# Attention tiles of a fused transformer block: residual rows moved from the GpSimd queue to the SyncE queue, weight loads paced by the attention tile before

## The chip, the cores and the metric

One Trainium2 chip, of which the kernel uses one core. The metric is the time of one execution on the device in microseconds (us); where several executions are shown, it is their median.

## The reference

One transformer block on 2048 tokens of width 1024, batch 1, weights and activations in bf16: a layer norm, linear attention with 32 heads of 32, a residual addition, a second layer norm, a gated MLP of width 3584, a second residual addition.

```
phi = lambda t: where(t > 0, t + 1, exp(t)) + 1e-6
q, k, v = heads(layernorm(x) @ wqkv)             # 32 heads of 32
kv = einsum("bhsd,bhse->bhde", phi(k), v);  z = phi(k).sum(s)
o  = (phi(q) @ kv) / (phi(q) . z + 1e-6)
h  = x + o @ wo
g  = layernorm(h) @ W_gate;  u = layernorm(h) @ W_up
out = h + (relu(g) * u) @ W_down
```

## The kernel before

The kernel runs through four stages. (1) K, V and the sums over tokens, to about 122 us: 16 tiles of 128 tokens are loaded, normalised, transposed by DMA and multiplied. (2) Q, the attention tiles and the first quarter of the MLP's up side (four column blocks for half of the tokens), to about 299 us. (3) The rest of gate and up, to about 585 us. (4) The down projection and the output. The large products use Strassen's scheme, seven products of blocks in place of eight, so the vector engine forms sums of input and weight blocks (`left_sums`, L113 to L120, and `weight_sums`, L606 to L620).

The change is in stage 2. `attn_stages(t)` (L497) makes five steps for one tile of 128 tokens:

- `nd` (L503 to L520): eight small matmuls (L511) give numerators and denominators, ACT inverts the denominators (L515, L517), DVE multiplies into `o_sb` (L518, three pieces for a tile).
- `oT` (L522 to L525): SyncE issues a DMA transpose of `o_sb`.
- `x_in` (L527 to L530): the tile's 128 rows of x (256 KB) are loaded into `x_res`, for the residual addition.
- `wo_h` (L532 to L557): sixteen matmuls with `wo` (L541), DVE adds x to them in place and sums the rows (L543, two pieces), the finished rows h are stored to `h_dram` (L546, 256 KB), DVE and ACT make mean and variance (L551 to L556; L553 is the pass that squares) and the normalised rows `hn` (L557).
- `hn_T` (L559, L560): SyncE issues a DMA transpose of `hn` into the operand of the MLP's matmuls. After tiles 4 to 7 and 12 to 15 `left_sums` follows on DVE.

The steps of different tiles overlap: `LAG = (0, 1, 1, 2, 4)` says by how many tiles each step trails `nd`. I number the tiles 0 to 15 in the order in which they run; oT(n), x(n), st(n) and hnT(n) are the transpose of `o_sb`, the load of x, the store of h and the transpose of `hn` of tile n.

Buffers set waits. `x_res` has three buffers (`XB = 3`), so x(n+3) may be issued only when st(n) has landed and L557 of tile n has read the buffer. `hn` has two (`HB = 2`), so the first pass over tile n+2 (L553) waits until hnT(n) has landed. `o_sb` has two.

The weights of the MLP's first four blocks, 4 MB in eight loads of 512 KB, arrive in the same stretch. `early_loads` (L486, issued by SyncE) are paced: before each, GpSimd copies one element of an `o_sb` into the destination (`hold`, L142), so that the load can't be issued before DVE has written that tile's `o_sb`. Step 1 issues two loads, steps 2 to 7 one each:

```
        if step:
            for _ in range(-(-len(early_loads) // (QSTEPS - step))):
                early_loads.pop(0)(held[step][0:1, 0:1])
```

The order on the engines is made by a scheduling framework: the program is recorded step by step, and the framework puts each engine's instructions into one fixed order, by its own estimate of when each could run. Every engine, and every engine's DMA issue queue, then works through its list in order: an instruction that waits holds up all behind it. So a changed issue engine can move instructions on other engines too.

Of the kernel before, what the change touches and what calls it, by code (L numbers as in the profile page):

```python
# [31 lines left out]
def block_kernel(ctx: ExitStack, tc: tile.TileContext, x, wqkv, wo, wg, wu, wd, out, H: int):  # L32
    nc = tc.nc
    P = 128
    xf = x.flatten_outer_dims()
# [35 lines left out]
    h_dram = [[dram.tile([P, NT, D], BF16, name=f"h_dram{i}_{s}") for s in range(NS)] for i in range(2)]  # L71
# [140 lines left out]
    with ExitStack() as actx:  # L212
# [208 lines left out]
        for c in range(KC):  # L421
            bnk, i = divmod(c, GPB)
# [54 lines left out]
    def load_group(g):  # L477

        tiles, loads = [], []
        for nm, v in (("wg", wg_v), ("wu", wu_v)):  # L480
            w_sb = wpools[g % 2].tile([P, KC, 2, GP * P], BF16, tag=nm, name=nm)
            for h in range(2):
                def load(after=None, w_sb=w_sb, v=v, h=h):
                    if after is not None:
                        hold(w_sb[0:1, 0, h, 0:1], after)
                    nc.sync.dma_start(out=w_sb[:, :, h, :], in_=v[:, :, h, g * GP * P:(g + 1) * GP * P])  # L486
                loads.append(load)
            tiles.append(w_sb)
        return tiles, loads

    early, early_loads = zip(*[load_group(g) for g in range(NE // GP)])
    early_loads = [f for loads in early_loads for f in loads]
    pieces = [(c, min(GPB, KC - c)) for c in range(0, KC, GPB)]

    held = []

    def attn_stages(t):  # L497

        i, r = divmod(t * P, HS)
        s, r = divmod(r, SW)  # L500
        st = {}

        def nd():  # L503
            o_sb = bwork.tile([P, D], BF16, tag="o_sb", name="o_sb")
            st["o"] = o_sb
            held.append(o_sb)
            ov = o_sb[:].rearrange("p (k h e) -> p k h e", k=KC, h=HPC)
            for c0, n in pieces:
                ps = ndpool.tile([P, NW], FP32, tag="ab", name="nd")
                for c in range(c0, c0 + n):  # L510
                    nc.tensor.matmul(ps[:, (c - c0) * NDW:(c - c0 + 1) * NDW], lhsT=pqT[:, c, t * P:(t + 1) * P],  # L511
                                     rhs=kvz[:, c, :], start=True, stop=True)
                ndv = ps[:, 0:n * NDW].rearrange("p (k w) -> p k w", w=NDW)
                den = bsmall.tile([P, GPB, HPC], FP32, tag="den", name="den")
                nc.scalar.activation(out=den[:, 0:n], in_=ndv[:, :, P:NDW], func=ACT.Ln, bias=deps[:], scale=1.0)  # L515
                rd = bsmall.tile([P, GPB, HPC], FP32, tag="rd", name="rd")
                nc.scalar.activation(out=rd[:, 0:n], in_=den[:, 0:n], func=ACT.Exp, scale=-1.0)  # L517
                nc.vector.tensor_tensor(  # L518
                    out=ov[:, c0:c0 + n], in0=ndv[:, :, 0:P].rearrange("p k (h e) -> p k h e", h=HPC),
                    in1=rd[:, 0:n, :].unsqueeze(3).to_broadcast([P, n, HPC, Dh]), op=ALU.mult)  # L520

        def oT():  # L522
            oT = bwork.tile([P, D], BF16, tag="oT", bufs=XB, name="oT")
            st["oT"] = oT[:].rearrange("p (c t) -> p c t", c=KC)
            nc.sync.dma_start_transpose(out=st["oT"], in_=st["o"][:])  # L525

        def x_in():  # L527
            x_sb = bwork.tile([P, D], BF16, tag="x_res", bufs=XB, name="x_res")
            nc.gpsimd.dma_start(out=x_sb[:], in_=xf[t * P:(t + 1) * P, :])
            st["x"] = x_sb  # L530

        def wo_h(borrow):  # L532
            h_sb = st["x"]
            tot = bsmall.tile([P, 2], FP32, tag="tot", name="tot")
            for j in range(2):
                if borrow:
                    ps = pspool.tile([P, NW], FP32, tag="E", bufs=2, name="attn")
                else:
                    ps = abpool.tile([P, NW], FP32, tag="ab", name="attn")
                for c in range(KC):  # L540
                    nc.tensor.matmul(ps[:], lhsT=st["oT"][:, c, :], rhs=wo_sb[:, c, j * NW:(j + 1) * NW],  # L541
                                     start=(c == 0), stop=(c == KC - 1))
                nc.vector.scalar_tensor_tensor(out=h_sb[:, j * NW:(j + 1) * NW], in0=ps[:], scalar=1.0,  # L543
                                               in1=h_sb[:, j * NW:(j + 1) * NW], op0=ALU.mult, op1=ALU.add,
                                               accum_out=tot[:, j:j + 1])
            nc.gpsimd.dma_start(out=h_dram[i][s][:, r // P, :], in_=h_sb[:])  # L546
            st["hn"] = bwork.tile([P, D], BF16, tag="hn", bufs=HB, name="hn")

            sm = bsmall.tile([P, 6], FP32, tag="sm", name="sm")
            nmean, var, lnv, rstd, nmr = (sm[:, i:i + 1] for i in range(5))  # L550
            nc.vector.tensor_scalar(out=nmean, in0=tot[:, 0:1], scalar1=tot[:, 1:2], scalar2=-1.0 / D,  # L551
                                    op0=ALU.add, op1=ALU.mult)
            nc.scalar.activation(out=st["hn"][:], in_=h_sb[:], func=ACT.Square, bias=nmean, scale=1.0, accum_out=var)  # L553
            nc.scalar.activation(out=lnv, in_=var, func=ACT.Ln, bias=LN_EPS, scale=1.0 / D)
            nc.scalar.activation(out=rstd, in_=lnv, func=ACT.Exp, scale=-0.5)
            nc.scalar.activation(out=nmr, in_=nmean, func=ACT.Identity, scale=rstd)  # L556
            nc.scalar.activation(out=st["hn"][:], in_=h_sb[:], func=ACT.Identity, bias=nmr, scale=rstd)  # L557

        def hn_T():  # L559
            nc.sync.dma_start_transpose(out=hnT[s][i][:, :, r:r + P], in_=st["hn"][:])  # L560

        return nd, oT, x_in, wo_h, hn_T

    LAG = (0, 1, 1, 2, 4)
# [5 lines left out]
    def attn_step(step):  # L570
        for k in range(len(LAG)):
            n = step - LAG[k]
            if n in begin_at:
                n = begin_at.index(n)
                if k == 3:
                    stages[n][k](QSTEPS <= step < STS + LAG[-1])
                else:
                    stages[n][k]()
                if k == len(LAG) - 1 and n % STS >= NT:
                    left_sums(hnT[n // STS], hns[n // STS], slice(n % NT * P, (n % NT + 1) * P), nc.vector)  # L580

    rest = [p for s in range(1, NS) for c in range(0, KH, 2) for p in [q_unit(s, c)] * 6]
    for step in range(QSTEPS):
        now = rest[step * len(rest) // QSTEPS:(step + 1) * len(rest) // QSTEPS]
        if step == QSTEPS - 1:
            while now:
                next(now.pop(0))
        attn_step(step)
        if step:
            for _ in range(-(-len(early_loads) // (QSTEPS - step))):  # L590
                early_loads.pop(0)(held[step][0:1, 0:1])
        for p in now:
            next(p)
    q1ctx.close()
# [285 lines left out]
    for r, (wt, f, fi, toks) in enumerate(runs):  # L880
        w = [ops() for _, ops in now]
        later = []
        for n, s in enumerate(toks):
# [51 lines left out]
            if k == nwin - 3:  # L935
                for x in range(2):
                    t = wpools[1].tile([P, KC * 2 * GP * P], BF16, tag=("wg", "wu")[x], name="wd")
# [16 lines left out]
    for n in range(2):  # L954
        t = fpool.tile([P, 4 * D], BF16, tag="wraw", bufs=2, name="xd")
# [242 lines left out]
    for n in range(1, len(OUTER)):  # L1198
# [73 lines left out]
        else:  # L1272
            pss = []
            for p in range(4):
# [13 lines left out]
                s, t0 = divmod(2 * p, NT)  # L1288
# [11 lines left out]
@with_exitstack  # L1300
def kernel(
    ctx: ExitStack,
    tc: tile.TileContext,
    A_x: bass.AP,
    A_wqkv: bass.AP,
    A_wo: bass.AP,
    B_x: bass.AP,
    B_W_gate: bass.AP,
    B_W_up: bass.AP,
    B_W_down: bass.AP,  # L1310
    out: bass.AP,
):
    block_kernel(tc, A_x, A_wqkv, A_wo, B_W_gate, B_W_up, B_W_down, out, H=32)
# [30 lines left out]
```

## Time and profile before

| | |
|---|---|
| median of 3 runs | 750.96 us (750.52 to 752.11) |
| the profiled execution | 750.52 us, its span 748.7 us |
| TensorE (PE) busy | 723.2 us, 97% of the span |
| VectorE (DVE), ScalarE (ACT), GpSimd (POOL) busy | 563.1, 322.4, 23.1 us |
| PE busy in 0 to 30 / 30 to 150 us | 25.63 / 117.07 us |
| PE busy in 150 to 290 us | 127.02 of 140 us |
| PE busy in 290 to 613 us | 321.60 of 323 us |
| x of the attention tiles, from GpSimd's queue | 16 loads of 256 KB, median 4.5 us to landing |
| h stores, from GpSimd's queue | 16 of 256 KB, median 3.5 us |
| oT and hnT, from SyncE's queue | 16 each, median 5.0 and 4.8 us |

How to read it: the matmuls fill the span almost everywhere. Time can be gained or lost only where PE has idle time or where something that PE waits for is late. In the attention stretch, between 150 and 290 us, PE is idle for about 13 us. After it, from 290 to 613 us, PE is idle for 1.4 us, so what that stretch loses or gains goes through to the end. The times from issue to landing include waiting behind other transfers on the 16 DMA engines.

### The profile page before, as it was taken

The numbers are of one execution on the slowest core, as the hardware profiler recorded it, in microseconds if no ns is written. First come the engines' busy times: TensorE is split into PE (matmuls) and PEld (weight loads), VectorE is DVE, ScalarE is ACT, GpSimd is POOL, SyncE is SP. The second block draws the span as 40 slices with busy tenths as digits, with TensorE's granted clock in tenths as the row PEclk, the third lists the DMA queues.
The fourth block names the chain that finished last, engine by engine and source line by source line (L and its number), as shares of the span: only waits on it lengthen the run. The fifth ranks groups of instructions, "written<-read, shape, count | busy, mean of one in ns | idle before, by whom it ended". The sixth has DMA issues, their size and how long they took to land.

```text
span 748.7 us, 10599 instructions
## 1 busy us (share of the span) xinstructions
PE 723.2 (97%) x3967; PEld 382.1 (51%) x4020; DVE 563.1 (75%) x991; ACT 322.4 (43%) x580; POOL 23.1 (3%) x76
## 2 busy tenths in 40 slices
PE   7999999999879989999999999999999999999997
PEld 3444555444434434444444444444444458888666
DVE  6997653775867568687787788877787469996797
ACT  4785653878577555444444344443435220000000
POOL 0000000011111000000000000000000000000000
PEclk9999999999999999999999999999999999999999
DMA  9765003079778635154837439466574299887822
GB/s 319 165 135 155 0 1 111 3 172 222 169 161 185 127 85 180 39 171 126 244 116 204 138 132 313 149 213 221 182 260 148 94 389 360 314 288 297 311 73 83
DMA packets 144532, 132.04 MB, mean 176 GB/s; under 512 B 50912, under 2 KB 128096, under 8 KB 144480
## 3 DMA queue, kind: packets, MB, share of 16 engines
q1 hardware_dynamic: 130784, 114.84, 51.4%
q0 software_dynamic: 2560, 8.39, 3.6%
q10 hardware_dynamic: 11136, 8.13, 3.4%
q8 instruction: 31, 0.51, 0.3%
q14 instruction: 21, 0.17, 0.1%
HBM read 79.95 MB, written 39.85 MB: 160 GB/s over the span
## 4 chain that ended last, share of the span: by engine, by line
PE 77%; DVE 8%; ACT 6%; DMA 6%; issue 2%; SPq 0%; DVEq 0%; POOL 0%; ACTq 0%
PE accA L785 22%; PE accX L785 8%; PE accY L785 8%; PE accA L1117 8%; DMA hn<-hn 3%; PE Aq L298 3%; PE accA L946 3%; PE Aq L438 3%; PE attn L541 3%; PE accX L1117 3%; PE accY L1117 2%; PE Eq L298 2%; PE accY L946 2%; PE accX L946 2%; PE Aq L705 1%
## 5 line engine op out<-in xcount | busy, mean ns | idle before, releaser
L795 ACT ACTIVATE gu<-gu 128x512 bf16<-128x512 bf16 x72 | 45.4, 630 | 131.2 <-DVE gu L794 131.2
L790 ACT COPY snap<-accA 128x1024 f32<-128x1024 f32 x72 | 72.5, 1008 | 36.6 <-PE accA L785 36.5
L541 PE MATMUL attn<-wo_mem,oT 128*128 128x512 bf16 x248 | 59.8, 386 | 5.6 <-DVE x_res L543 3.7
L785 PEld LDWEIGHTS <-tg 128*128 128x128 f16 x384 | 37.5, 98 | 45.3
L785 PEld LDWEIGHTS <-tu 128*128 128x128 f16 x384 | 37.5, 98 | 45.4
L794 DVE TENSOR_TENSOR gu<-accY,snap 128x1024 bf16<-128x1024 f32 x36 | 43.9, 1219 | 10.0 <-ACT snap L790 10.0
L785 PE MATMUL accA<-hn,tg 128*128 128x512 f16 (+1 forms) x192 | 49.3, 379 | 0.0
L785 PE MATMUL accA<-hn,tu 128*128 128x512 f16 (+1 forms) x192 | 49.3, 379 | 0.0
L154 ACT COPY u<-Aq 128x512 f32<-128x512 f32 x56 | 32.3, 582 | 38.5 <-PE Aq L298 20.0
L794 DVE TENSOR_TENSOR gu<-accX,snap 128x1024 bf16<-128x1024 f32 x36 | 43.9, 1219 | 6.5 <-PE accX L785 3.7
L1117 PEld LDWEIGHTS <-x 128*128 128x128 f16 (+1 forms) x448 | 43.8, 98 | 5.6
L785 PEld LDWEIGHTS <-wg 128*128 128x128 bf16 x288 | 28.2, 98 | 34.0
L785 PEld LDWEIGHTS <-wu 128*128 128x128 bf16 x288 | 28.1, 98 | 34.0
L541 PEld LDWEIGHTS <-oT 128*128 128x128 bf16 x256 | 24.9, 99 | 35.0 <-issue 4.9
L798 DVE TENSOR_TENSOR hq<-gu 128x512 bf16<-128x512 bf16 x48 | 20.3, 423 | 14.3 <-ACT gu L795 14.2
L298 PEld LDWEIGHTS <-xT 128*128 128x128 bf16 (+1 forms) x192 | 18.6, 98 | 24.4 <-issue 3.0
L1117 PEld LDWEIGHTS <-xs 128*128 128x128 f16 x280 | 27.3, 98 | 3.4
L543 DVE SCALAR_TENSOR_TENSOR x_res<-attn,x_res 128x512 bf16<-128x512 f32 x32 | 21.9, 687 | 8.6 <-PE attn L541 8.6
L946 PEld LDWEIGHTS <-x 128*128 128x128 bf16 (+1 forms) x168 | 16.4, 98 | 19.6
L518 DVE TENSOR_TENSOR o_sb<-nd,rd 128x384 bf16<-128x384 f32 (+1 forms) x48 | 22.6, 506 | 4.4 <-ACT rd L517 4.4
L1123 DVE TENSOR_TENSOR snap<-accA,u 128x1024 f32<-128x1024 f32 x16 | 19.5, 1219 | 8.4 <-PE accA L1117 8.3
L785 PE MATMUL accA<-hs,tg 128*128 128x512 f16 x96 | 24.6, 379 | 0.0
(234 smaller groups left out, 1418.4 us busy)
## 6 DMA issues: line engine op xcount, KB each, us to landing
x<-x_dram SPq DMA_DIRECT2D x17, 896.0 KB, 8.5
x_dram<-hq SPq DMA_DIRECT2D x28, 512.0 KB, 3.3
wg<-in_B_W_gate_dram SPq DMA_DIRECT2D x14, 512.0 KB, 5.4
wu<-in_B_W_up_dram SPq DMA_DIRECT2D x14, 512.0 KB, 7.2
wraw<-in_B_W_down_dram SPq DMA_DIRECT2D x14, 512.0 KB, 4.9
x_dram<-hq SPq DMA_DIRECT2D x28, 256.0 KB, 2.8
t_dram<-wt SPq DMA_DIRECT2D x28, 256.0 KB, 2.2
xd<-x_dram SPq DMA_DIRECT2D x6, 896.0 KB, 7.0
```

The lines of the kernel that those rows point to most:

```text
L154: nc.scalar.copy(out=snaps[nm, v], in_=A[v][:])
L298: nc.tensor.matmul(ps[:], lhsT=left[m - 1][:, kc, r + v * P:r + (v + 1) * P], rhs=right[m - 1][:, kc, :], start=(start and kc == 0), stop= ...
L438: nc.tensor.matmul(ps[:], lhsT=rq[m - 1][:, kc, (c + v) * P:(c + v + 1) * P], rhs=left[m - 1][:, kc, :], start=(start and kc == 0), stop=( ...
L518: nc.vector.tensor_tensor(out=ov[:, c0:c0 + n], in0=ndv[:, :, 0:P].rearrange("p k (h e) -> p k h e", h=HPC), in1=rd[:, 0:n, :].unsqueeze(3 ...
L541: nc.tensor.matmul(ps[:], lhsT=st["oT"][:, c, :], rhs=wo_sb[:, c, j * NW:(j + 1) * NW], start=(c == 0), stop=(c == KC - 1))
L543: nc.vector.scalar_tensor_tensor(out=h_sb[:, j * NW:(j + 1) * NW], in0=ps[:], scalar=1.0, in1=h_sb[:, j * NW:(j + 1) * NW], op0=ALU.mult, ...
L785: nc.tensor.matmul(ps[:, v, :], lhsT=w[v][n - 1][:, kc, :], rhs=left[n - 1][:, kc, :], start=(t is not None and kc == 0), stop=(kc == KH - ...
L790: nc.scalar.copy(out=st[nm][:], in_=halves(st["A"]))
L794: add(out=g[:], in0=halves(st[nm]), in1=st[base][:], op=ALU.add)
L795: nc.scalar.activation(out=g[:, 0, :], in_=g[:, 0, :], func=ACT.Relu)
L946: nc.tensor.matmul(ps[:, t * NW:(t + 1) * NW], lhsT=x_tile(n, s, kh)[:, f, (t0 + t) * P:(t0 + t + 1) * P], rhs=w_tile(n, kh)[:, f, :], sta ...
L1117: nc.tensor.matmul(pv[:, tt, :], lhsT=left(m)[:, f, tt * P:(tt + 1) * P], rhs=right(m)[:, f, :], start=(t is not None and f == 0 and tt % ...
```

## The change

Loads of x and stores of h in the attention tiles are issued by SyncE in place of GpSimd, and the early weight loads are paced by the `o_sb` of the tile before.

```diff
         def x_in():
             x_sb = bwork.tile([P, D], BF16, tag="x_res", bufs=XB, name="x_res")
-            nc.gpsimd.dma_start(out=x_sb[:], in_=xf[t * P:(t + 1) * P, :])
+            nc.sync.dma_start(out=x_sb[:], in_=xf[t * P:(t + 1) * P, :])
             st["x"] = x_sb
...
-            nc.gpsimd.dma_start(out=h_dram[i][s][:, r // P, :], in_=h_sb[:])
+            nc.sync.dma_start(out=h_dram[i][s][:, r // P, :], in_=h_sb[:])
             st["hn"] = bwork.tile([P, D], BF16, tag="hn", bufs=HB, name="hn")
...
             for _ in range(-(-len(early_loads) // (QSTEPS - step))):
-                early_loads.pop(0)(held[step][0:1, 0:1])
+                early_loads.pop(0)(held[step - 1][0:1, 0:1])
```

Built, the two programs have the same work on each engine, but for GpSimd's 32 DMA issues, which are now among SyncE's. In SyncE's list x(n+3), and often st(n+1), now stand between oT(n+3) or oT(n+4) and hnT(n). The orders on PE, DVE and ACT agree up to the eighth attention tile and differ in places between it and the end of the attention stretch; from there on they agree again.

## The prediction

> **What bounds the kernel now.** I began with the busy times and the table by stretches. PE is busy for 97% of the span, and its idle time sits in the attention stretch. Columns: stretch, then busy time (count) of PE, weight loads, DVE, ACT and POOL, the granted TensorE clock, the DMA engines' busy share, GB/s.
>
> ```profile
> PE 723.2 (97%) x3967; PEld 382.1 (51%) x4020; DVE 563.1 (75%) x991; ACT 322.4 (43%) x580; POOL 23.1 (3%) x76
> ...
> 170.00:180.00 10.00, 9.95 (x52) 4.73 (x52) 6.91 (x18) 8.88 (x22) 1.43 (x4) 1.00 1.01 233
> 180.00:190.00 10.00, 8.66 (x46) 4.12 (x46) 4.87 (x11) 7.79 (x19) 1.78 (x4) 1.00 0.88 202
> ...
> 200.00:210.00 10.00, 7.17 (x44) 3.66 (x44) 8.03 (x24) 4.53 (x17) 1.10 (x3) 1.00 0.75 198
> 210.00:220.00 10.00, 6.29 (x37) 3.12 (x35) 5.25 (x17) 6.55 (x21) 1.62 (x3) 0.95 0.89 170
> ...
> 260.00:270.00 10.00, 8.33 (x39) 3.68 (x39) 8.19 (x21) 4.66 (x9) 0.55 (x1) 1.00 0.41 86
> ```
>
> Four holes in PE's work matter: 1.3 us at 186, 2.8 at 204 to 207, 3.7 at 215 to 219, 1.7 at 264. The chain that ended last says what closes them (start, length, what):
>
> ```profile
> 175.52 6.14 DMA hn<-hn
> 181.76 1.24 ACT hn L553 x2
> ...
> 201.59 5.56 DMA oT<-o_sb
> 207.19 0.61 PE attn L541 x2
> ...
> 210.00 6.54 DMA hn<-hn
> 216.57 0.42 DVE hs L117
> ...
> 218.34 0.62 DVE x_res L543 x2
> 219.00 1.01 PE attn L541 x2
> ...
> 221.57 4.43 DMA hn<-hn
> ...
> 256.12 5.42 DMA hn<-hn
> ```
>
> The reader is to see that each hole hangs on a DMA transpose, four of the five on an hnT: numbers 1, 5, 7 and 12. hnT(1) holds up ACT, which waits for its buffer before L553 of tile 3. hnT(5) and hnT(12) hold up DVE, which waits in L117 with later work behind it. A transpose with no company lands in 3.1 us (hnT 13, 14 and 15), so about half of these links is waiting for other transfers.
>
> SyncE's own list shows what goes ahead of them:
>
> ```profile
> 196.00:198.00 2.00, 1.95 (x10) 0.90 (x10) 2.00 (x5) 2.00 (x8) 0.00 (x0) 1.00 0.00 0
> ...
> 204.00:206.00 2.00, 0.08 (x1) 0.00 (x0) 1.00 (x4) 0.42 (x1) 0.00 (x0) 1.00 1.16 320
> ...
> 199.05 0.37 SPq L486 DMA_DIRECT2D wu<-in_B_W_up_dram  x1
> 199.52 1.98 SPq L560 DMA_TRANSPOSE hn<-hn  x1
> ```
>
> The last weight load is issued at 199.05, just ahead of hnT(4), after 3 us in which the DMA engines did nothing.
>
> **The change, part by part.** *Removed from GpSimd:* 32 issues of 0.54 us, 17.3 of its 23.1 us. No hole of PE names GpSimd, so this is worth nothing by itself.
>
> *Added to SyncE:* 32 issues. A row load of the same shape from SyncE (L226) takes 0.51 to 0.54. A store of this shape isn't there; the nearest, `raw_dram`, takes 0.33 to 0.53. I take 0.54 for both, 17.3 us in all. Three loads fall in the first stage. SyncE is idle from 53.9 to 59.1, which covers two of them (1.1 us; without it, the wq load on the chain at 61.24 would be that much later), and from 67.8 to 123.0, which covers the third. The buffers that they wait for belong to tiles whose transposes stand ahead of them in the list, so they add no wait. Cost nothing.
>
> The other 29 fall between 150 and 290. SyncE has the time: what counts is what they stand in front of. x(n+3) waits for st(n) to land and for L557 of tile n. Behind it stands hnT(n), which needs the same L557; so hnT(n) comes 0.54 later, and 1.08 where a store stands there too. Behind hnT stand L553 two tiles on and, for tiles 4 to 7 and 12 to 15, L117. Link by link:
>
> - *hnT(1):* the built list has oT(4), x(4), st(2), hnT(1). Issue goes from 175.52 to 176.6, 1.1 later. The same 512 KB were beside it before (issued at 175.03 and 175.64), so the landing may absorb it: 0 to +1.1, and +1.6 if x(4) must also wait for st(1). I take +0.7, nearer to the issue row. It goes through ACT to PE's hole at 186.
> - *hnT(5):* x(8) ahead of it, +0.54. Before, it took 6.5 us: beside it ran x(8), and st(7), x(9) and oT(9) that were issued after it, two of them on GpSimd's queue. On one queue the later ones stand behind. hnT(10) and hnT(11), each with one row load issued just after, took 4.5 and 4.4. I go three quarters of the way, to 5.0: -1.5 + 0.5 = -1.0. Ends: +0.5 (no faster landing) and -2.9 (3.1, alone).
> - *hnT(7):* x(10) and st(8) stand ahead, 1.08 us. Before, it waited behind oT(10) anyway, issued 1.6 us after its L557. I take +0.3, ends 0 and +1.1.
> - *hnT(12):* x(15) ahead, +0.5. But the built order also moves DVE's second L714 of that block, which stood behind L117 and kept PE waiting 1.67 us, ahead of L117. Its input is ready at 261.6, PE needs it at 263.6. So -1.67 + 0.5, about -1.1. Ends: -1.7, and +1.1 if DVE stalls elsewhere.
> - The other hnT (0, 2, 3, 6, 8 to 11, 13 to 15) come 0.5 to 1.9 later. The two-buffer wait behind them has cover: L553 of tile 4 starts 5.6 us after hnT(2) landed, that of tile 10 3.2 us after hnT(8). A second, larger delay would reach PE.
>
> *The pacing:* each hold now reads the `o_sb` before. Its first pieces are written at 150.4, 153.8, 157.6, 164.2, 171, 176 and 188 (L518), so the loads go at about 151, 154.6, 157, 158, 164.5, 171, 180 (behind oT(5) on SyncE) and 188.5, where before they went at 154.65, 155.2, 159.2, 164.5, 171.0, 176.9, 188.7 and 199.05. The eighth leaves 199 and the first takes a stretch (150 to 154) in which the DMA engines are idle. Nobody waited for any of them. Ahead of hnT(4) and oT(7) there are then 256 KB, x(7), in place of 768. hnT(4) took 5.5, or 2.4 over the quiet 3.1; a third of that leaves 3.9. Issued at 199.18 + 0.54, it lands at 203.7 in place of 205.0, where DVE's L117 had waited 1.95. oT(7) gains about 2. The nearer limit is DVE's: -1.3. Ends 0 and -1.95.
>
> Sum: 0.7 - 1.0 + 0.3 - 1.1 - 1.3 = -2.4 us. The profiled execution took 750.52 (748.7 of span, 1.8 around it), so 748.1. The median lies 0.44 above that execution: 748.6.
>
> One rule speaks against the third term. The Trainium skill, "DMA: Bandwidth & Descriptors", section "Issuing engines are not separate DMA queues", says that transfers from all issuing engines interleave on the same 16 DMA engines, and that issuing from several saves only the sequencer's time, usually small. By it hnT(5) would land no sooner for the move, its term would be +0.5, and the sum -0.9, for 750.1. I go by the rows, hnT(5) at 6.5 against 4.5 for its likes, since their company differed.
>
> **The rivals.** *SyncE's list becomes the bound (slower).* One mechanism: hnT(n) behind x(n+3) and st(n+1), with no shorter landing. Place: hnT 1, 5, 7 and 12, the four links of the chain. Price 1.08 each, +4.3, with the gain at 199 taken back by the same wait on hnT(4): 755.3. It decides as soon as the landings stay at 6.1, 6.5, 4.4 and 5.4, because these links have no slack: their waiters idled until they landed. For it: SyncE's transposes already take up to 3.7 us to issue between 155 and 192 when the DMA engines are full, and 29 issues more feed the same queue. Against it: after 230 the tiles are some 10 us apart, and SyncE idles between them.
>
> *Nothing to be seen.* The holds move loads that nobody waited for, SyncE issues in order anyway, and 1.1 of gain meets 1.1 of loss: 751.0. For it: PE's holes move from one link to the next when one is shortened, as the five different links show.
>
> *A larger gain.* The hole at 215 to 219 is followed by a slow clock: 0.73 in 218 to 220, 0.50 in 220 to 222, 0.92 in 222 to 224, which costs 0.54 + 1.0 + 0.16 = 1.7 us. The built order puts four matmuls of the MLP (L705, 1.0 us) into that hole and lets two L518 go ahead of L543. If the hole closes so far that the clock holds, a further 2.7 us: 748.6 - 2.7 = 745.9. Against it: PE's next wait, at 226, hangs on hnT(7), which is issued 5.1 us after hnT(5) lands in either order, so PE would only wait there.
>
> **How the numbers follow.** The forecast (a gain of 1.5 to 4 us) has 0.36, the larger gain 0.14, nothing 0.18, slower 0.32. I give the slower case so much because three of the five terms rest on landings that become shorter, which no row shows for this order. All low ends together give -6.5, all high ends +4.3: 744.5 to 755.3. I take 744.5 to 755.0 for 8 times in 10; the forecast's own range is 747.0 to 749.5. A change of 0.2%, 1.5 us, is about what a measurement of this kernel can tell from none. Faster by more: 0.36 + 0.14 = 0.50; within: 0.18; slower: 0.32.
>
> **What would show it.** Right: PE busy in 200 to 210 above 8 us; hnT(4) landing before 204.5; no weight load after 190; hnT(5) in 5 us or less; no wait of PE for L714 near 264. Wrong: hnT landings as long as before with issues 0.5 to 1.1 later; PE's hole at 186 longer than 2.5 us; SyncE waiting for st(n) to land with hnT(n) behind it; a new hole of PE before 180. If PE waits for attention tile 0 near 157, the first weight load has delayed oT(0), which I put at nothing (before, it landed 1.1 us ahead of its matmul).

## The result, and the profile after

The changed kernel takes 744.33 us (median of 4 runs, 744.15 to 745.94), the kernel before 750.74 us in the same comparison. The ratio is 0.9916, 95% interval 0.9897 to 0.9935: a gain of 6.4 us, where 2.4 were forecast. The profiled execution took 745.94 us, with a span of 744.1. It lies 1.6 us above the median, so the two traces show 4.6 us of the gain (span 748.7 to 744.1).

The busy times of the changed kernel:

```profile
PE 724.6 (97%) x3967; PEld 382.2 (51%) x4020; DVE 563.0 (76%) x991; ACT 322.0 (43%) x580; POOL 5.6 (1%) x44
```

and its table by stretches, columns as in the prediction:

```profile
150.00:160.00 10.00, 9.24 (x55) 4.46 (x55) 6.94 (x15) 6.04 (x21) 1.05 (x4) 1.00 0.73 161
180.00:190.00 10.00, 8.78 (x47) 4.18 (x47) 4.93 (x11) 7.71 (x19) 0.18 (x1) 1.00 0.94 203
200.00:210.00 10.00, 9.66 (x60) 4.94 (x60) 9.66 (x29) 6.81 (x30) 0.00 (x0) 1.00 0.77 169
210.00:220.00 10.00, 8.15 (x45) 3.85 (x44) 7.01 (x22) 7.25 (x22) 0.00 (x0) 1.00 1.27 238
260.00:270.00 10.00, 9.22 (x43) 4.15 (x43) 8.31 (x23) 6.31 (x14) 0.00 (x0) 1.00 0.36 106
```

PE is busier by 2.5 us in 200 to 210 (7.17 before) and by 1.9 in 210 to 220 (6.29). By longer stretches, before and after: 150 to 200, 48.22 and 47.65; 200 to 220, 13.46 and 17.81; 220 to 260, 38.59 and 37.81; 260 to 290, 26.75 and 28.75. So the gain is made in two places, 200 to 220 and 260 to 290. In 150 to 160 PE is busy 0.71 us less than before (9.95).

The chain that ended last:

```profile
177.44 4.88 DMA hn<-hn
...
182.43 1.24 ACT hn L553 x2
...
200.25 3.69 DMA hn<-hn
...
211.82 0.58 SPq L529
...
212.46 5.39 DMA hn<-hn
...
217.87 0.42 DVE hs L117
...
222.30 1.01 PE Eq L705 x2
...
263.11 3.05 DMA hn<-hn
```

It still runs over hnT, but over other ones: 1, 4, 6 and 13. hnT(5) and hnT(12), which had 6.54 and 5.42 us in the chain before, are no longer in it. hnT as a whole came down from a median of 4.8 us to 3.6, and DVE's wait for it in L117 was halved (total us, times, longest), before and after:

```profile
DVE hs L117 <- DMA hn<-hn: 12.9, 6, 3.8
```

```profile
DVE hs L117 <- DMA hn<-hn: 6.9, 6, 3.0
```

SyncE's list around hnT(4) in the changed kernel:

```profile
189.60 0.53 SPq L486 DMA_DIRECT2D wu<-in_B_W_up_dram  x1
...
199.87 0.33 SPq L529 DMA_DIRECT2D x_res<-in_A_x_dram  x1
200.25 1.24 SPq L560 DMA_TRANSPOSE hn<-hn  x1
```

The last weight load is now at 189.60, x(7) stands ahead of hnT(4), and hnT(4) lands in 3.7 us (5.5 before). Two things have changed here at once, the weight load and the queue of x(7), and the order on DVE besides; this trace can't say which of them counts.

### The profile page after: what moved, and what is told of

The parts are those of the page before. It is cut to its first block, busy times and chain, and to the rows that moved or that the text cites. A ratio compares the mean times of both kernels' runs of the same rounds, so it can differ in the third digit from the quotient of the medians.

```text
span 744.1 us, 10568 instructions
## 1 busy us (share of the span) xinstructions
PE 724.6 (97%) x3967; PEld 382.2 (51%) x4020; DVE 563.0 (76%) x991; ACT 322.0 (43%) x580; POOL 5.6 (1%) x44
## 4 chain that ended last, share of the span: by engine, by line
PE 80%; DVE 8%; ACT 6%; DMA 4%; issue 1%; SPq 0%; DVEq 0%; ACTq 0%
PE accA L785 22%; PE accY L785 8%; PE accX L785 8%; PE accA L1117 8%; PE Aq L298 4%; PE accA L946 3%; PE attn L541 3%; PE accX L1117 3%; PE Aq L438 3%; DMA hn<-hn 3%; PE accY L1117 2%; PE Eq L298 2%; PE Aq L705 2%; PE accY L946 2%; PE accX L946 2%
## 5 line engine op out<-in xcount | busy, mean ns | idle before, releaser
L785 PEld LDWEIGHTS <-tu 128*128 128x128 f16 x384 | 37.5, 98 | 45.3
L785 PEld LDWEIGHTS <-tg 128*128 128x128 f16 x384 | 37.5, 98 | 45.4
L541 PE MATMUL attn<-wo_mem,oT 128*128 128x512 bf16 x249 | 57.9, 379 | 1.6 <-DVE o_sb L518 1.1
L785 PE MATMUL accA<-hn,tu 128*128 128x512 f16 (+1 forms) x192 | 49.3, 379 | 0.0
L785 PE MATMUL accA<-hn,tg 128*128 128x512 f16 (+1 forms) x192 | 49.3, 379 | 0.0
L785 PEld LDWEIGHTS <-wu 128*128 128x128 bf16 x288 | 28.2, 98 | 34.0
L785 PEld LDWEIGHTS <-wg 128*128 128x128 bf16 x288 | 28.1, 98 | 34.0
L543 DVE SCALAR_TENSOR_TENSOR x_res<-attn,x_res 128x512 bf16<-128x512 f32 x32 | 21.8, 688 | 8.6 <-PE attn L541 8.5
L785 PE MATMUL accA<-hs,tu 128*128 128x512 f16 x96 | 24.6, 379 | 0.0
```

The source lines that it names most:

```text
L785: nc.tensor.matmul(ps[:, v, :], lhsT=w[v][n - 1][:, kc, :], rhs=left[n - 1][:, kc, :], start=(t is not None and kc == 0), stop=(kc == KH - ...
```

## The experiments

The ratios are to runs of the kernel before on the same chip. In the diffs, + and - are against the kernel that the sentence names.

**One part alone (against before).** The changed kernel makes three edits; four kernels make one or two of them.

```diff
-                early_loads.pop(0)(held[step][0:1, 0:1])
+                early_loads.pop(0)(held[step - 1][0:1, 0:1])
```

> Only the pacing is changed; x and h stay on GpSimd's queue, and the order on PE and ACT is that of before. If the pacing is the main part (it takes the eighth weight load out of the way of hnT(4)), PE busy in 200 to 210 rises from 7.17 to about 9.5 and the time falls by 2 to 3 us, to about 748.3. If the queues are the main part, the landings of hnT stay at a median near 4.8 us and the time falls by 1.3 us at most (749.4 to 751).

Measured: 753.12 us, ratio 1.0034 (1.0016 to 1.0052). The pacing alone costs some 2.6 us. The eighth weight load is out of the way, and hnT(4) is none the shorter; SyncE's list of this kernel, and then its chain:

```profile
189.50 0.37 SPq L486 DMA_DIRECT2D wu<-in_B_W_up_dram  x1
...
200.15 1.23 SPq L560 DMA_TRANSPOSE hn<-hn  x1
```

```profile
200.15 5.94 DMA hn<-hn
```

Besides, the order built for DVE now has L117 of tile 4 ahead of a second L543, so that DVE waits 3.10 us in L117 with that L543 behind it, and PE waits 2.9 us for the L543.

The two queues alone:

```diff
-            nc.gpsimd.dma_start(out=x_sb[:], in_=xf[t * P:(t + 1) * P, :])
+            nc.sync.dma_start(out=x_sb[:], in_=xf[t * P:(t + 1) * P, :])
...
-            nc.gpsimd.dma_start(out=h_dram[i][s][:, r // P, :], in_=h_sb[:])
+            nc.sync.dma_start(out=h_dram[i][s][:, r // P, :], in_=h_sb[:])
```

> Only the queues are changed; the pacing is that of before. If the queues are the main part, the landings of hnT fall to a median near 3.7 us, the time is 745 to 747 and what is missing to the changed kernel (744.3) is the stretch 200 to 210, where hnT(4) still stands behind the eighth weight load. If the pacing is the main part, the time is 748.5 or more.

Measured: 744.18 us, ratio 0.9915 (0.9885 to 0.9945), hnT median 3.7. That is the whole gain, and the stretch that was to be missing isn't: PE is busy for 9.51 us in 200 to 210. SyncE's list, and the landing of the hnT(4) in it:

```profile
199.97 0.38 SPq L486 DMA_DIRECT2D wu<-in_B_W_up_dram  x1
200.44 0.53 SPq L529 DMA_DIRECT2D x_res<-in_A_x_dram  x1
...
202.75 1.64 SPq L560 DMA_TRANSPOSE hn<-hn  x1
```

```profile
DMA to landing us min/median/max: 4.0/4.0/4.0
```

This must be read with care. In this list oT(7), too, goes ahead of hnT(4), which is issued 2.8 us after the weight load and lands at 206.75, later than before (204.98). DVE waits for it for only 0.31 us (1.95 before), since the order built puts L117 of tile 4 later on DVE. So the full stretch 200 to 210 goes here with the order built, and not with an earlier hnT(4). What x(7) does to hnT(4) shows where neither kernel has a weight load near it: 5.9 us with x(7) from GpSimd (pacing alone), 3.7 with x(7) from SyncE (the changed kernel). A weight load right ahead counts as well: of the two kernels further below that record x behind hnT, the one that issues such a load 0.43 us ahead of hnT(4) has a hnT(4) of 4.6 us, the other, without one there, 3.1.

The first of these two edits alone:

> Only the loads of x go to SyncE. PE and ACT have the same order as with both moved, and DVE nearly. If the built order brings the gain, the time equals that of the kernel with both queues moved, within 1 us. If the landings bring it, stores on GpSimd's queue still lengthen the transposes behind them: hnT median about 4.3 us and about half of the gain.

Measured: 744.33 us, ratio 0.9912 (0.9887 to 0.9938), hnT median 3.6. The second alone:

> Only the stores of h go to SyncE; DVE and ACT have the order of before, PE an order of its own. If the landings bring the gain, the median landing of hnT falls from 4.8 to about 4.3 us and the time by 1 to 3 us (748 to 750). If only the order that comes with x on SyncE brings it, 750 to 752; and if stores ahead of hnT(n) on one queue cost their issue and their transfer, up to 753.

Measured: 750.55 us, ratio 0.9997 (0.9979 to 1.0015), hnT median 5.0. So the loads of x carry everything and the stores nothing. But with x on SyncE, PE's order is another, too.

**Which loads (against before).** Two x loads on SyncE, and the mirror image, with the other fourteen in the list:

```diff
-            nc.gpsimd.dma_start(out=x_sb[:], in_=xf[t * P:(t + 1) * P, :])
+            (nc.sync if order.index(t) in (7, 8) else nc.gpsimd).dma_start(
+                out=x_sb[:], in_=xf[t * P:(t + 1) * P, :])
```

> Before, with two of the sixteen x loads (tiles 7 and 8) on SyncE. Built, PE, DVE and ACT have exactly the order of the kernel with all x loads on SyncE; fourteen loads and all stores stay on GpSimd's queue. If the built order brings the gain: 744.3 us, within 1 us. If the shorter landings bring it: 749 us or more, with a median landing of hnT of 4.4 us or more, since fourteen loads still run beside the transposes from a second queue.

Measured: 745.87 us, ratio 0.9958 (0.9940 to 0.9976), hnT median 5.1.

> The mirror image: fourteen x loads on SyncE, those of tiles 7 and 8 on GpSimd. Built, PE has exactly the order of before (DVE and ACT differ from before in one place, near tile 12). If the built order brings the gain: 749 to 751 us, with PE waiting 3 us or more between 215 and 220 for DVE, however short the landings are. If the landings bring it: hnT median 3.9 us or less and 745 to 747 us.

Measured: 746.05 us, ratio 0.9947 (0.9927 to 0.9967), hnT median 3.6. These are gains of 0.42% and 0.53%, where the changed kernel gains 0.84%. The first lies between its two expectations, the second is what was expected if the landings bring the gain. The single transposes say why. This is hnT(5) when x(8) is on SyncE, and then when it is on GpSimd:

```profile
L560 SPq DMA_TRANSPOSE hn<-hn x1: 1237/1237/1237, 207.8 to 207.8; - x1
...
DMA to landing us min/median/max: 3.7/3.7/3.7
```

```profile
L560 SPq DMA_TRANSPOSE hn<-hn x1: 1232/1232/1232, 208.7 to 208.7; - x1
...
DMA to landing us min/median/max: 6.1/6.1/6.1
```

x(7) is issued beside hnT(4) and x(8) beside hnT(5). In the first kernel these two take 3.8 and 3.7 us, and hnT 6, 8, 10, 11 and 12 take 5.8 to 6.4; in the second, hnT(4) and hnT(5) take 5.4 and 6.1, and from hnT(6) on all take 4.1 or less. Each load switches the transpose beside it:

| kernel | x loads | hnT median | hnT(4) | hnT(5) | PE busy 200 to 220 | time |
|---|---|---|---|---|---|---|
| before | GpSimd | 4.8 | 5.5 | 6.5 | 13.46 | 750.74 |
| pacing alone | GpSimd | 4.4 | 5.9 | 6.9 | 15.11 | 753.12 |
| stores alone | GpSimd | 5.0 | 5.2 | 6.6 | 14.65 | 750.55 |
| x(7), x(8) on SyncE | mixed | 5.1 | 3.8 | 3.7 | 17.95 | 745.87 |
| x(7), x(8) on GpSimd | mixed | 3.6 | 5.4 | 6.1 | 15.72 | 746.05 |
| x alone | SyncE | 3.6 | 4.7 | 3.7 | 17.56 | 744.33 |
| both queues | SyncE | 3.7 | 4.0 | 3.4 | 18.70 | 744.18 |
| changed | SyncE | 3.6 | 3.7 | 3.6 | 17.81 | 744.33 |

The kernels "x(7), x(8) on SyncE" and "x alone" have the same order on PE, DVE and ACT. The other fourteen loads make the difference between them (ratios 0.9958 and 0.9912).

A third kernel was to put eight loads of the changed kernel back:

> The changed kernel with the x loads of tiles 5 to 12 back on GpSimd; PE, DVE and ACT keep exactly its order. These are the loads that run beside hnT(2) to hnT(9). If the built order brings the gain: 744.3 us, within 1 us. If the landings bring it: hnT(4) to hnT(7) take 4.5 to 6.5 us again and the time goes to 748 us or more.

Measured: 755.98 us, ratio 1.0089 (1.0063 to 1.0115). It isn't the kernel that the expectation describes: the edit also took hold in L226, whose text is the same, and put eight of stage 1's sixteen loads on GpSimd, and PE's order is not that of the changed kernel either. Stage 2 begins 7.0 us later in it (129.81 in place of 122.81), so its time says nothing on the question. (Its hnT(4) and hnT(5), with x(7) and x(8) from GpSimd, took 5.8 and 6.4 us.)

**Transposes lengthened in the order that the change built (against the changed kernel).** First a further store of `hn` beside the transpose. In the first kernel it is made for tiles 4 and 5 alone, in the second for all sixteen, and the control issues all sixteen from SyncE behind hnT.

```diff
             nc.sync.dma_start_transpose(out=hnT[s][i][:, :, r:r + P], in_=st["hn"][:])
+            nc.gpsimd.dma_start(out=x_copy[t][:], in_=st["hn"][:])
```

> The changed kernel with one further transfer beside hnT(4) and one beside hnT(5): the rows hn, 256 KB, are also stored from GpSimd's queue to memory that nobody reads, released by the same L557 as the transpose. Built, PE, DVE, ACT and SyncE have exactly the order of the changed kernel, so only the landings can differ. If a transfer from GpSimd's queue beside the transpose is what made the landings long: hnT(4) and hnT(5) take 5.5 to 6.5 us in place of 3.7 and 3.6, DVE waits for them, and the time goes from 744.3 to 746.5 to 748. If the built order made the gain, and the order keeps it: 744.3 to 745.

Measured: 745.10 us, ratio 0.9925 (0.9907 to 0.9943). hnT(4) and hnT(5) took 4.2 and 4.3, so they were hardly lengthened, and the run decides little.

> The same beside all sixteen hnT, the order again exactly that of the changed kernel. If the landings carry the gain: median landing of hnT 5 us or more in place of 3.6, and 749 to 753 us, the whole gain gone in the order that the change built. If the built order carries it: below 746.5.

Measured: 751.56 us, ratio 1.0007 (0.9991 to 1.0023), hnT median 4.4 (less than expected): the whole gain is gone, with PE, DVE and ACT in the order that the change built.

> The control: the same sixteen further stores, issued by SyncE right behind each hnT (PE, DVE and ACT get an order of their own). If it is the second queue that lengthens the transposes, and not the bytes: hnT median 4.2 us or less and a time within 2 us of the changed kernel. If it is the bytes: as with the copies from GpSimd.

Measured: 743.98 us, ratio 0.9905 (0.9887 to 0.9923), hnT median 3.5. DVE's wait for hnT (the lines of the code stand one lower in these two, so it is L118), with the copies from GpSimd and then from SyncE:

```profile
DVE hs L118 <- DMA hn<-hn: 15.9, 7, 4.6
```

```profile
DVE hs L118 <- DMA hn<-hn: 5.5, 4, 3.1
```

The same 4 MB cost 7 us from one queue and nothing from the other.

Then a further load, like those that the change moved, into a tile that nobody reads; first for tiles 4 and 5, then with SyncE as the issuing engine, then for all sixteen, and last for tiles 4 and 5 with the store as well:

```diff
             nc.sync.dma_start_transpose(out=hnT[s][i][:, :, r:r + P], in_=st["hn"][:])
+            if order.index(t) in (4, 5):
+                hold(x_extra[0:1, 0:1], st["hn"][0:1, 0:1])
+                nc.gpsimd.dma_start(out=x_extra[:], in_=xf[t * P:(t + 1) * P, :])
```

> The changed kernel with one further load of 256 KB of x from GpSimd's queue beside hnT(4) and one beside hnT(5), into a tile that nobody reads, each released by the same L557 as the transpose (through a one-element copy on GpSimd). PE, DVE, ACT and SyncE have exactly the order of the changed kernel. A store from that queue had made these two only 0.5 and 0.7 us longer; before, with x(7) and x(8) there, they took 5.5 and 6.5. If it is a load from the second queue that makes them long: 5 to 6.5 us each, PE busy in 200 to 220 down from 17.8 to about 15.5, and 746 to 748 us. If the built order makes the gain in that stretch: above 17 and 745.5 or less.

Measured: 747.43 us, ratio 0.9954 (0.9936 to 0.9972); hnT(4) 4.7, hnT(5) 4.4 (shorter than expected), PE busy 17.38 in 200 to 220.

> The control: the same two loads from SyncE's queue, each behind its hnT. PE and ACT keep the order of the changed kernel, DVE too but for four instructions near tile 7. If the queue and not the bytes makes the transposes long: hnT(4) and hnT(5) 4.3 us or less and a time within 1 us of the changed kernel.

Measured: 746.66 us, ratio 0.9946 (0.9930 to 0.9961); hnT(4) 3.4, hnT(5) 3.6. The control is 2.3 us slower than the changed kernel, against its expectation, and the two intervals overlap, so this pair decides nothing by its times. In the traces stage 2, from the first matmul of L438 to the first of L785, lasts 171.6 us in the changed kernel, 172.0 in the control and 173.4 with the loads from GpSimd. There the loads cost nearly 2 us from GpSimd and 0.5 from SyncE, in one execution each. Most of the control's loss lies outside stage 2, and I haven't found its cause.

> Such a load from GpSimd's queue beside all sixteen hnT, the order exactly that of the changed kernel. If the landings carry the whole gain: hnT median 5 us or more and 751 us or more. If the order carries part of it: 747 to 750.

Measured: 756.15 us, ratio 1.0063 (1.0045 to 1.0080), hnT median 4.5 (less than expected). This is slower than the kernel before, whose median was 4.8, so the median alone doesn't give the time.

> The changed kernel with both a load of x and a store of hn (256 KB each) from GpSimd's queue beside hnT(4) and hnT(5); PE, DVE, ACT and SyncE have its order exactly. If the landings carry the gain: these two take 5.5 us or more, PE busy in 200 to 220 falls below 16.5 (17.8 in the changed kernel, 17.4 with the load alone), and 748 to 750. If the order carries it: as with the load alone, 747.4.

Measured: 749.14 us, ratio 0.9987 (0.9975 to 1.0000). hnT(4) and hnT(5) took 5.7 and 5.4, PE was busy for 15.56 us in 200 to 220, and DVE waits for both again (one line lower in the code, L118):

```profile
204.90 0.43 DVE L118 TENSOR_TENSOR hs<-hn 128x512 f16<-128x512 bf16 x1 [2.20 <-DMA hn<-hn]
...
214.83 0.42 DVE L118 TENSOR_TENSOR hs<-hn 128x512 f16<-128x512 bf16 x1 [2.45 <-DMA hn<-hn]
```

Four transfers from GpSimd beside two transposes take back 4.8 of the 6.4 us, the order unchanged. The control's unexplained 2.3 could be in that time, but little of it is in stage 2, which lasts 175.5 us here, some 4 more than in the changed kernel (before the change, 176.4); the control's is 0.5 longer.

**The reverse: the order of a kernel that gained nothing, with short transposes.** x is recorded behind hn_T (against the changed kernel); in the second kernel the pacing is that of before as well.

```diff
-        for k in range(len(LAG)):
+        for k in (0, 1, 3, 4, 2):
```

> The changed kernel with x(n+3) recorded behind hnT(n), so that in SyncE's list the load no longer stands in front of the transpose that needs the same L557. If the 0.5 us of issue and the load's bytes ahead of hnT still count: hnT 0.5 us earlier and 742 to 744. If the load comes too late for L543 or the order made is worse: 745 to 748.

Measured: 742.02 us, ratio 0.9884 (0.9867 to 0.9902), hnT median 3.1: faster than both kernels.

> Loads of x and stores of h on SyncE, x(n+3) recorded behind hnT(n), the pacing of before. Built, DVE and ACT have exactly the order of before, and PE, DVE and ACT exactly that of the kernel with the stores alone on SyncE, which took 750.55 (ratio 0.9997): the two differ only in the queue of the x loads. If the landings carry the gain: hnT median near 3.1 us, PE busy in 200 to 220 above 17 (there 14.66) and 742 to 744.5. If the order that came with x on SyncE carried it: 748 or more.

Measured: 741.97 us, ratio 0.9895 (0.9878 to 0.9912), hnT median 3.4. PE, DVE and ACT run the same lists here as in the kernel with the stores alone on SyncE, and SyncE's list differs by the x loads alone. DVE's waits for hnT(5) and hnT(12) there, and then PE's idle times (in brackets, with what ended them):

```profile
214.41 0.42 DVE L117 TENSOR_TENSOR hs<-hn 128x512 f16<-128x512 bf16 x1 [3.90 <-DMA hn<-hn]
...
260.24 0.43 DVE L117 TENSOR_TENSOR hs<-hn 128x512 f16<-128x512 bf16 x1 [3.96 <-DMA hn<-hn]
```

```profile
216.84 0.38 PE L541 MATMUL attn<-wo_mem,oT 128*128 128x512 bf16 x1 [3.41 <-DVE x_res L543]
...
263.92 1.02 PE L705 MATMUL Eq<-hs,wu 128*128 128x512 f16 x4 [2.56 <-DVE gu L714]
```

and here:

```profile
209.15 0.43 DVE L117 TENSOR_TENSOR hs<-hn 128x512 f16<-128x512 bf16 x1 [0.31 <-DMA hn<-hn]
...
252.34 0.43 DVE L117 TENSOR_TENSOR hs<-hn 128x512 f16<-128x512 bf16 x1 [0.71 <-DMA hn<-hn]
```

```profile
212.97 0.39 PE L541 MATMUL attn<-wo_mem,oT 128*128 128x512 bf16 x1 [1.32 <-DVE x_res L543]
...
219.64 0.59 PE L705 MATMUL Eq<-hs,tg 128*128 128x512 f16 x2 [1.63 <-DVE hs L117]
...
264.84 1.02 PE L705 MATMUL Aq<-hs,tu 128*128 128x512 f16 x4 [0.36 <-ACT m L154]
```

hnT(5) took 6.6 us there and 3.1 here, hnT(12) 6.3 and 3.1. PE's hole of 3.41 us shrank to 1.32 and that of 2.56 is gone, without any instruction of these three engines being moved; the wait for L117 at 219 grew (1.63, 0.47 there). PE busy in 200 to 220 came to 15.88 us, less than the 17 expected, with holes of 1.06, 1.32 and 1.63 us in it, and the next ten microseconds are full (9.92). The queue of sixteen loads makes 8.6 us by the medians, 7.7 by the ratios (0.9997 to 0.9895).

**What is left over.** One more try at the changed kernel: `left_sums` recorded one step later, at the next step's hn_T.

```diff
                 if k == len(LAG) - 1 and n % STS >= NT:
-                    left_sums(hnT[n // STS], hns[n // STS], slice(n % NT * P, (n % NT + 1) * P), nc.vector)
+                    due.append(n)
```

> The changed kernel with left_sums of a tile recorded one step later, so that on DVE more L543 and L518 stand ahead of L117 and the wait for hnT holds up less. If DVE's waits in L117 are what is left of the holes (2.4 us at 217.9 and what follows to 226): 741 to 743. If the sums then come too late for L705: 745 to 748.

Measured: 744.98 us, ratio 0.9918 (0.9898 to 0.9939): as the changed kernel. DVE's waits for hnT in L117 came down from 6.9 us to 3.3, but PE waits 2.1 us for L117 in place of 1.28, so this later place of L117 gains nothing.

## Why the prediction was wrong in size

The direction and the place were right, and every sign named as "right" came: PE busy 9.66 us in 200 to 210, hnT(4) landed at 203.9, no weight load after 190, hnT(5) in 3.6, no wait for L714 near 264. The sum was 2.4 and should have been 6.4. By stretches it had 0.7 us lost ahead of 200, 2.3 gained in 200 to 220, 0.3 lost in 220 to 260 and 1.1 gained after that; in PE's busy time the traces have 0.57 lost, 4.35 gained, 0.78 lost and 2.00 gained. The failed step is the pricing of the landings: each term took its shorter landing from something else, or not at all, and the one cause behind all of them, the x loads on a second queue beside the transposes, was priced in one term only, and there at a half.

- *hnT(5), priced -1.0.* "I go three quarters of the way, to 5.0." It landed in 3.6, near the end that I had called "alone" (3.1). Issued 1.5 us earlier and 3.0 shorter, it let DVE's L117 start at 212.06 in place of 216.57: 4.5 us, where the terms for hnT(4) and hnT(5) together had 2.3. I had named the right mechanism (company on GpSimd's queue) and chosen hnT(10) and hnT(11) as its likes; they had a GpSimd load beside them as well, so they weren't the quiet case.
- *The pacing, priced -1.3.* The number came out by luck (hnT(4) in 3.7, 3.9 forecast), for the cause was wrong. "Ahead of hnT(4) and oT(7) there are then 256 KB, x(7), in place of 768" counted bytes. Pacing alone took the weights away and x(7) stayed on GpSimd: it costs 2.6 us and leaves hnT(4) at 5.9. The queues alone leave the weights there, and 200 to 210 is full all the same, with hnT(4) landing later than before. Given the queues, the pacing is worth nothing either way (744.33 and 744.18; 742.02 and 741.97). In the traces with the new pacing PE waits 0.9 us or more for `o_sb` ahead of the attention matmuls, with the old one 0.6 or less; in the changed kernel that is a hole of 0.71 at 158.4, where oT(0) had landed at 157.7. So it wasn't oT(0), the sign that I had named, and why `o_sb` is later stays open. The sum had put this part of the pacing at nothing.
- *hnT(12) and L714, priced -1.1.* 260 to 290 gained 2.0. I gave this to the built order and let the landing stay long. With that order and a hnT(12) of 5.9 us (x(7), x(8) on SyncE) PE is busy for 8.21 us in 260 to 270, as before (8.33), and waits 2.6 us for ACT; with the same order and a hnT(12) of 3.5 (x alone) it is busy for 9.27; with the order of before on DVE and a hnT(12) of 3.1 the wait for L714 shrinks to 0.2. The landing carries this term, too.
- *hnT(1), priced +0.7.* L553 of tile 3 starts at 182.43 in place of 181.76, 0.7 later: hnT(1) was issued 1.9 later and took 1.3 less. The size agrees by luck. PE was already 0.7 late from the hole at 158, and its hole at 186 did not grow (1.29 before, 1.16 after). So this term cost nothing, and the 0.57 us that PE lost in 150 to 200 goes with the pacing (48.72 with the queues alone, 47.45 with the pacing alone), which the sum had at nothing there.
- *hnT(7), priced +0.3.* It is issued at 217.21, 5.15 us after hnT(5) landed, as I had said of either order; landing in 3.9 in place of 4.4. From hnT(5)'s landing to its own it was 9.5 us before and 9.0 after, so the link itself cost nothing in place of 0.3. PE's wait for L117 moved from 226.5 to 222.3 and grew from 0.66 to 1.28 us, since PE came there sooner.
- *Of the rivals,* the larger gain was nearest in time (745.9), but not by its mechanism: the clock fell again, as the rows of the changed kernel show in the column before the last two.

```profile
220.00:222.00 2.00, 0.89 (x8) 0.53 (x8) 2.00 (x7) 1.93 (x6) 0.00 (x0) 0.91 0.37 80
222.00:224.00 2.00, 1.70 (x5) 0.59 (x5) 2.00 (x7) 1.94 (x8) 0.00 (x0) 0.50 0.72 145
224.00:226.00 2.00, 2.00 (x8) 0.79 (x7) 1.90 (x5) 1.00 (x4) 0.00 (x0) 0.74 1.32 311
```

- The slow clock has only moved behind the holes of 1.39 and 1.28 us at 220 and 222; the larger gain came from landings. In the two fastest kernels this dip is absent (1.00 in 220 to 230), which can be part of their further 2 us. SyncE's list, the slower rival, did not become the bound: hnT was issued 0.7 to 2 us later up to hnT(4), and shorter landings outweighed it. That x(n+3) stands in front of hnT(n) may still cost: recorded behind it, the kernel gains 2.3 us more and the hnT median falls to 3.1, though in an order of its own on PE and DVE.

The rule that I had weighed, in the Trainium skill, "DMA: Bandwidth & Descriptors", section "Issuing engines are not separate DMA queues" (transfers from all engines share the DMA engines, and spreading them saves issue time only), would have had hnT(5) land no sooner. The runs differ: 3.6 against 6.5 us, and some 8 us of kernel time, for the queue of the loads alone. The same page, section "Queues, rings and completion order", says that each DMA engine takes turns between the queues that have work, a whole packet at a time. That fits a transpose that is slowed by a load on a second queue and not by one behind it in its own; no run here looks into the turns themselves. Nor does a run issue the loads from a third engine: the profile lists GpSimd's queue as software_dynamic (2560 packets, 8.39 MB before) and SyncE's as hardware_dynamic, which grows by 4608 packets for the same bytes. Whether any second queue would do the same, or only GpSimd's, stays open.

The traces explain 4.6 of the 6.4 us; the other 1.8 lie between the two profiled executions and the medians (1.6 after, 0.2 before), where no trace was taken.

## What to carry to other kernels

Where a chain hangs on short DMA transposes, look at which queue the transfers beside them come from before counting their bytes: on the transposes' own queue a neighbour ahead costs its place in the list (with a weight load just ahead, 4.6 us in place of 3.1) and one behind costs nearly nothing, on GpSimd's queue it cost landing time here (6.5 us against 3.6 for hnT(5)). Then put the transpose ahead of what doesn't hurry. And when a change moves two things at once and each sign that you listed fits both, the signs can't tell you which one counted; make one part alone.

## What was not expected of the hardware

One load and one transpose of 256 KB each, issued within half a microsecond, finish sooner from one queue than from two. Before, x(8) left GpSimd 0.3 us after hnT(5) left SyncE:

```profile
L529 POOL DMA_DIRECT2D x_res<-in_A_x_dram x1: 541/541/541, 210.3 to 210.3; - x1
...
DMA to landing us min/median/max: 5.7/5.7/5.7
```

and in the changed kernel x(8) leaves SyncE 0.45 us ahead of hnT(5):

```profile
L529 SPq DMA_DIRECT2D x_res<-in_A_x_dram x1: 404/404/404, 208.0 to 208.0; - x1
...
DMA to landing us min/median/max: 3.0/3.0/3.0
```

From the first issue to the last landing, both together took 6.5 us before (210.00 to 216.54) and 4.0 after (208.01 to 212.03). They weren't alone: st(7), oT(9) and x(9) were issued before hnT(5) landed in both, the two of them that GpSimd had issued now from SyncE as well. One further transfer from that queue in the changed kernel did much less: beside hnT(4) and hnT(5) one store left them at 4.2 and 4.3 us, one load at 4.7 and 4.4, both at 5.7 and 5.4. That is one traced execution each, and beside all sixteen the medians are 4.4 with stores and 4.5 with loads, so a difference between stores and loads isn't shown. Moving the sixteen h stores off that queue alone shortened nothing (hnT median 5.0).
